# Lightning attention and a Mish feed-forward in one kernel: the place of two "turns" of group 3, and of one key decay in the head

## The chip, the cores and the metric

The kernel runs on one core of a Trainium2 chip. The metric is the device time of one execution in microseconds (us); several executions are timed and their median is given. A profile is one more execution, recorded by the hardware profiler. The engines are called PE (matrix multiplication; PEld is its weight load), DVE (VectorE), ACT (ScalarE), POOL (GpSimd) and SP (SyncE, which only issues DMAs here). ACT and POOL issue DMAs too, each in its own instruction order: a DMA whose conditions are not met holds up everything behind it on the issuing engine.

## The reference

Four batches, eight heads, 768 positions, head size 64. Causal attention without softmax and with a decay per head goes block by block over the positions and carries a 64 x 64 state per head; its result, laid out as 3072 tokens x 512, goes through a feed-forward layer with the Mish function. Cut to what matters:

```python
for b in range(nb):                          # blocks of positions
    intra = einsum('bhic,bhjc->bhij', qb, kb) * Dmask
    intra = einsum('bhij,bhjd->bhid', intra, vb)
    inter = einsum('bhid,bhde->bhie', qb * lam_pow, kv_state)
    out[:, :, sl] = intra + inter
    kv_state = lam_block * kv_state + einsum('bhsd,bhse->bhde', kb * rev_pow, vb)
x = out.transpose(0, 2, 1, 3).reshape(3072, 512)
h = x @ w_in                                 # 512 -> 2048
g = h * tanh(softplus(h))                    # Mish
return g @ w_out                             # 2048 -> 512
```

## The kernel before

**Groups and chunks.** The 768 positions are cut into six groups of 128 (`n`, 0 to 5; the "fourth group" is n = 3). A group has four chunks, one per batch: chunk `i = 4 n + b` is 128 positions of batch `b`, all eight heads. Below, k12 or q12 means the key or query part of chunk 12, v12 its values; chunks 12 to 15 are group 3.

**Attention of a chunk.** `load_k`, `load_q`, `load_v` (L62 to L79) fetch a chunk from HBM as fp16; POOL issues them. `scale_k` (L263) multiplies the keys by their decay and gives `ktil`; it runs on POOL for groups 1 to 4 and on DVE for groups 0 and 5. Groups 0 and 1 are transposed on PE (`first_t`, `first_s`, `first_o`); `first_t(c)` of group 1 reads `ktil`. From group 2 on, `turn(i)` (L270) does the same job by DMA: `scale_k(i)`, then two transposing DMAs issued by SP, `qn` to `qraw` and `ktil` to `kraw` (L275). `pair_s` (L312) multiplies `kraw` by `qraw` for two chunks at a time, `pair_o` (L342) forms the attention output, and SP issues two more transposing DMAs from `xtok` into `xt` (L361), the layout that the feed-forward reads. `pair_a` updates the state: PE, then DVE (`raw`), then POOL (`w`, L305).

**Feed-forward of a group.** `mm1_unit` (L383) makes one 128 x 512 piece of the hidden layer in a PSUM tile `ph` (two buffers) and ACT applies Mish into `hsg` (L387). `mm2_unit` (L429) makes a quarter of one batch's output in `po`; after the fourth quarter ACT copies `po` to `osb` (L427, three buffers) and itself issues the output DMA (L424, 256 KB). Both instructions stand on ACT, one behind the other.

**Periods.** After a head in which groups 0 and 1 go through attention and `mm1`, the main loop (L533) runs n = 1 to 5. A period is a list of "units" of feed-forward work on PE (n = 1: the 32 `mm2_unit`s of groups 0 and 1; n = 2 to 5: 16 `mm1_unit`s, then 16 `mm2_unit`s), and `todo` (filled by `at`) says what is put behind which unit: the attention of group n+1 (`pair_s`, `pair_o`, `pair_a`), and the loads and turns of group n+2. Nothing is reordered later: what each engine does stands in the order in which this code is written out. Loads are held back by `behind` (L367), a one-element POOL copy from a result that must be there first ("tick").

**DMA names.** The DMAs that SP and ACT issue take eight completion semaphores in turn, in program order. A DMA that takes a semaphore waits until the DMA that had it before has landed. In the instruction lists below, `DMAHW5_49` among an instruction's waits is such a semaphore, and `DMASW...` those of the loads.

**The head's loads.** Behind the weights, POOL issues the twelve loads of group 1 (L487 to L493) with the key decays of its chunks between them (`scale_k(B)` is chunk 4), then the loads of `w_out` and the first loads of group 2.

Of the kernel before, what the change touches and what calls it, by code (L numbers as in the profile page):

```python
# [13 lines left out]
def bc(ap, axis, n):  # L14
    shape = list(ap.shape)
    shape.insert(axis, n)
    return ap.unsqueeze(axis).broadcast_to(shape)
# [3 lines left out]
def kernel(  # L21
# [11 lines left out]
    B, H, S, D = q.shape  # L33
# [9 lines left out]
    NVB = 8  # L43
    NT = 2
# [13 lines left out]
    def chunk_rows(t, i):  # L58
        n, b = divmod(i, B)
        return t[b, :, n * C : (n + 1) * C, :].rearrange("h p c -> p h c")  # L60

    def load_k(i):  # L62
        if i == 0:
            kn[i] = const.tile([128, H, D], F32, name="kn0")
            nc.sync.dma_start(out=kn[i], in_=chunk_rows(k, i))
            return
        kn[i] = loads.tile([128, H, D], F16, name="kn", tag="kn")
        nc.gpsimd.dma_start(out=kn[i], in_=chunk_rows(k, i))  # L68

    def load_q(i):  # L70
        if i == 0:
            qn[i] = const.tile([128, H, D], F32, name="qn0")
            nc.scalar.dma_start(out=qn[i], in_=chunk_rows(q, i))
            return
        qn[i] = loads.tile([128, H, D], F16, name="qn", tag="qn")
        nc.gpsimd.dma_start(out=qn[i], in_=chunk_rows(q, i))  # L76

    def load_v(i):
        nc.gpsimd.dma_start(out=vz[i % NVB][:, :, 0:D], in_=chunk_rows(v, i))  # L79
# [32 lines left out]
    def load_chunk(i):  # L112
        load_k(i)
        load_q(i)
        load_v(i)
# [147 lines left out]
    def scale_k(i):  # L263

        t = work.tile([128, H, D], F16, name="ktil", tag="ktil", bufs=8)
        (nc.vector if i < B or i >= (NG - 1) * B else nc.gpsimd).tensor_tensor(  # L266
            out=t, in0=kn[i], in1=bc(lk, 2, D), op=ALU.mult)
        ktil[i] = t
# [98 lines left out]
    def behind(src):  # L367
        nc.gpsimd.tensor_copy(tick, src)  # L368

    hsg = [None] * NG  # L370
# [113 lines left out]
    for hp in range(2):  # L484
        rs = slice(64 * hp, 64 * hp + 64)
        nc.vector.tensor_copy(lbm[rs, :, rs], bc(lbc[rs, :], 2, D))
    for i in range(B, NVB - 1):  # L487
        load_chunk(i)
    scale_k(B)
    load_k(NVB - 1)  # L490
    scale_k(B + 1)
    load_q(NVB - 1)
# [11 lines left out]
    for u in range(NKI):  # L504
# [7 lines left out]
        if u in (6, 7, 8, 10):  # L512
            i = {6: 4, 7: 5, 8: 6, 10: 7}[u]
# [19 lines left out]
    for n in range(NT - 1, NG):  # L533
        dense = [(mm2_unit, m, b, part) for m in ((0, 1) if n < NT else (n,))
                 for b in range(B) for part in range(WS)]
        if n >= NT:
            dense = [(mm1_unit, n, ni) for ni in range(NKI)] + dense
        todo = {}

        def at(u, f, *args):  # L540
            todo.setdefault(u, []).append((f, args))

        if n + 1 < NG:
            pairs = []
            for b in (0, 2):
                s = Pair()
                s.n, s.b = n + 1, b
                pairs.append(s)
            steps = (((9, pair_s, 0), (13, pair_o, 0), (14, pair_a, 0),
                      (16, pair_s, 1), (20, pair_o, 1), (28, pair_a, 1)) if n < NT else  # L550
                     ((4, pair_s, 0), (8, pair_o, 0), (9, pair_a, 0),
                      (13, pair_s, 1), (17, pair_o, 1), (25, pair_a, 1)))
            for u, f, b in steps:
                at(u, f, pairs[b])
        if n + 2 < NG:
            c = (n + 2) * B
            loads_ = [(f, c + b) for b in range(B) for f in (load_k, load_q)]
            loads_ += [(load_v, c + b) for b in range(B)]
            for x, (f, i) in enumerate(loads_):
                if n >= NT:  # L560
                    u = (1, 2, 3, 5, 6, 8, 10, 11, 12, 13, 14, 15)[x]
                    at(u, lambda u=u: behind(hsg[n][0:1, u, 0:1]))
                else:
                    u = 7 + x // 2 * 4
                    if x % 2 == 0:
                        at(u, lambda: behind(last_out[0][0:1, 0:1]))
                at(u, f, i)
            for b, u in enumerate((21, 22, 24, 26) if n < NT else (18, 19, 21, 23)):
                at(u, turn, c + b)
        for u, (fn, *args) in enumerate(dense):  # L570
            fn(*args)
            for f2, args in todo.get(u, ()):
                if args and isinstance(args[0], Pair):
                    args[0].spare = "po" if u < NKI - 1 and n >= NT else "ph"
                f2(*args)
# [30 lines left out]
```

## Time and profile before

| | |
|---|---|
| time, median of 3 runs | 214.5 us (213.99, 214.5, 215.1) |
| the profiled execution's own time | 214.28 us |
| its span in the profile | 212.5 us |
| granted PE clock | 1.0 |
| PE busy | 203.4 us, 96% of the span |
| POOL, ACT, DVE busy | 112.8, 86.3, 72.4 us |

All times inside the profile count from the start of the span. The span is 1.78 us shorter than the execution's time. Matmul ends in the profile are modelled, so a stall of PE is best read from starts. Period n = 1 begins at about 55 us, n = 2 at 86.15 us, n = 3 at 119.6 us.

### The profile page before, as it was taken

What the parts mean: (1) busy time and instruction counts of PE and PEld (TensorE: products, weight loads), DVE (VectorE), ACT (ScalarE), POOL (GpSimd) and SP (SyncE); (2) the same over time, 40 slices, a digit from 0 to 9 for tenths busy, and PEclk for the clock granted to TensorE, in tenths of its full rate; (3) what the DMA queues carried; (4) which work ended last, traced back from release to release, by engine and by line L of the source; (5) the groups of instructions that cost most, each with busy time, mean ns of one, the idle gap of its engine ahead of it and who ended that gap; (6) DMA issues with size and microseconds to landing.
All of it is one profiled execution on the core that took longest, in us unless ns stands there. A gap on an engine that the chain in (4) does not pass through costs nothing.

```text
span 212.5 us, 4185 instructions
## 1 busy us (share of the span) xinstructions
PE 203.4 (96%) x1680; PEld 111.4 (52%) x1680; DVE 72.4 (34%) x149; ACT 86.3 (41%) x146; POOL 112.8 (53%) x166
## 2 busy tenths in 40 slices
PE   7798999999999999699999999999999999999994
PEld 2465547999645545255454455545454544444442
DVE  6867736740005822044422044462042510000000
ACT  5664566656321121355412355412356321566120
POOL 7997399989934879768994169924000000000000
PEclk9999999999999999999999999999999999999999
DMA  9999999999999999999998799997702042100112
GB/s 130 138 150 192 187 155 116 185 187 156 145 169 233 147 132 174 165 232 87 108 142 201 181 91 86 107 180 156 193 10 47 2 102 99 51 0 0 52 49 99
DMA packets 109894, 26.76 MB, mean 126 GB/s; under 512 B 102578, under 2 KB 106930, under 8 KB 109874
## 3 DMA queue, kind: packets, MB, share of 16 engines
q0 software_dynamic: 78080, 13.37, 84.4%
q1 hardware_dynamic: 27296, 6.63, 19.4%
q10 hardware_dynamic: 4498, 6.49, 9.4%
q8 instruction: 13, 0.21, 0.4%
q14 instruction: 7, 0.06, 0.1%
HBM read 27.26 MB, written 6.29 MB: 158 GB/s over the span
## 4 chain that ended last, share of the span: by engine, by line
PE 77%; POOL 10%; DMA 8%; issue 2%; ACT 1%; DVE 0%; ACTq 0%; POOLq 0%
PE po L412 34%; PE ph L380 27%; PE ph L398 6%; DMA win<-in_moe_w_in_dram 6%; DMA kraw<-ktil 3%; POOL vz L79 3%; PE pS L324 2%; POOL qn L76 2%; PE pO L351 2%; POOL kn L68 2%; PE pv L291 1%; POOL ktil L266 1%; POOL win L92 1%; PE pO L330 1%; PE pO L256 1%
## 5 line engine op out<-in xcount | busy, mean ns | idle before, releaser
L412 PE MATMUL po<-wout,hsg 128*128 128x512 f16 (+2 forms) x400 | 85.6, 371 | 0.0
L380 PE MATMUL ph<-xt,win 128*128 128x512 f16 (+2 forms) x332 | 73.9, 371 | 2.3 <-ACT hsg L387 2.1
L387 ACT ACTIVATE hsg<-ph 128x512 f16<-128x512 f32 x80 | 47.5, 597 | 31.3 <-PE ph L380 30.5
L412 PEld LDWEIGHTS <-hsg 128*128 128x128 f16 x400 | 37.9, 98 | 41.9
L380 PEld LDWEIGHTS <-win 128*128 128x128 f16 x332 | 30.8, 98 | 36.3 <-issue 3.4
L427 ACT ACTIVATE osb<-po 128x512 f32<-128x512 f32 (+1 forms) x24 | 14.2, 593 | 75.5 <-PE po L412 65.1
L339 DVE TENSOR_TENSOR sb<-pS,maskT 128x512 f16<-128x512 f32 x32 | 19.9, 682 | 52.6 <-PE pS L324 52.6
L305 POOL TENSOR_TENSOR w<-raw,lbm 128x256 f16<-128x256 f32 x32 | 22.2, 724 | 10.8 <-DVE raw L303 10.7
L68 POOL DMA_DIRECT2D kn<-in_k_dram x23 | 21.2, 923 | 4.0 <-DMA win<-in_moe_w_in_dram 1.7
L79 POOL DMA_DIRECT2D vz<-in_v_dram x24 | 21.6, 904 | 2.0 <-DMA win<-in_moe_w_in_dram 2.0
L76 POOL DMA_DIRECT2D qn<-in_q_dram x23 | 20.7, 901 | 3.6 <-DMA win<-in_moe_w_in_dram 1.6
L303 DVE TENSOR_TENSOR raw<-pv,w 128x256 f32<-128x256 f32 x32 | 11.4, 414 | 16.4 <-PE pv L291 16.4
L266 POOL TENSOR_TENSOR ktil<-kn,lk 128x512 f16<-128x512 f16 x16 | 16.5, 1052 | 0.3
L357 DVE TENSOR_TENSOR xtok<-pO,lqt 128x512 f16<-128x512 f32 x16 | 10.3, 686 | 15.9 <-PE pO L351 15.9
L398 PE MATMUL ph<-xt,win 128*128 128x128 f16 x256 | 15.3, 219 | 0.0
L398 PEld LDWEIGHTS <-win 128*128 128x128 f16 x256 | 14.5, 98 | 0.1
L421 DVE COPY osb<-po 128x128 f32<-128x128 f32 x1 | 0.3, 291 | 38.7 <-PE po L412 38.7
L402 ACT ACTIVATE hsg<-ph 128x512 f16<-128x512 f32 x16 | 9.6, 597 | 6.9 <-PE ph L398 6.9
L368 POOL COPY tick<-hsg 1x1 f16<-1x1 f16 x24 | 4.2, 177 | 8.7 <-ACT hsg L387 8.6
L163 PE MATMUL busy<-kzero 128*128 128x512 f16 x18 | 7.6, 516 | 1.2 <-DVE kzero L149 1.2
L291 PEld LDWEIGHTS <-ktil 128*128 128x128 f16 x80 | 5.5, 98 | 2.7 <-issue 0.3
L291 PE MATMUL pv<-vz,ktil 128*128 128x128 f16 x80 | 6.8, 219 | 0.2 <-DVE sb L241 0.2
(68 smaller groups left out, 117.2 us busy)
## 6 DMA issues: line engine op xcount, KB each, us to landing
out_dram<-osb ACTq DMA_DIRECT2D x23, 256.0 KB, 3.0
vz<-in_v_dram POOLq DMA_DIRECT2D x24, 128.0 KB, 4.8
kn<-in_k_dram POOLq DMA_DIRECT2D x23, 128.0 KB, 4.2
qn<-in_q_dram POOLq DMA_DIRECT2D x23, 128.0 KB, 4.4
wout<-in_moe_w_out_dram POOLq DMA_DIRECT2D x4, 512.0 KB, 8.7
win<-in_moe_w_in_dram POOLq DMA_DIRECT2D x3, 512.0 KB, 10.3
kn<-in_k_dram SPq DMA_DIRECT2D x1, 256.0 KB, 3.2
qn<-in_q_dram ACTq DMA_DIRECT2D x1, 256.0 KB, 3.9
```

Of the source, the lines that this page charges most:

```text
L68: nc.gpsimd.dma_start(out=kn[i], in_=chunk_rows(k, i))
L76: nc.gpsimd.dma_start(out=qn[i], in_=chunk_rows(q, i))
L79: nc.gpsimd.dma_start(out=vz[i % NVB][:, :, 0:D], in_=chunk_rows(v, i))
L266: (nc.vector if i < B or i >= (NG - 1) * B else nc.gpsimd).tensor_tensor(out=t, in0=kn[i], in1=bc(lk, 2, D), op=ALU.mult)
L291: nc.tensor.matmul(pv[:, j, :].rearrange("p (a e) -> p a e", a=2), ktil[i][:, 2 * j : 2 * j + 2, :].rearrange("p h c -> p (h c)"), vz[i % ...
L305: nc.gpsimd.tensor_tensor(out=w_new, in0=raw, in1=lbm[:, hs, :], op=ALU.mult)
L339: nc.vector.tensor_tensor(out=s.sb[x][t], in0=pS[x][t], in1=bc(maskT, 1, JP), op=ALU.mult)
L380: nc.tensor.matmul(ph_t[ni][:, lo:hi], win_t(ni, kc), xt[n][:, kc, lo:hi], start=(kc == 0), stop=(kc == NKC - 1))
L387: nc.scalar.activation(hsg[n][:, ni, :], ph_t.pop(ni), AF.Mish)
L398: nc.tensor.matmul(ph[:, u, :], win_t(w * s + u, kc), xt[n][:, kc, b * C : (b + 1) * C], start=(kc == 0), stop=(kc == NKC - 1),)
L412: nc.tensor.matmul(po[:, lo:hi], hsg[n][:, ki, b * C : (b + 1) * C], wout[part][:, kk, lo:hi], start=(ki == 0), stop=(ki == NKI - 1),)
L427: nc.scalar.activation(o, i, AF.Copy)
```

## The change

Two edits.

1. In period n = 1 the four turns of group 3 stood behind units 21, 22, 24 and 26. Now only the first two (chunks 12 and 13) stand there, behind units 21 and 23. The other two (chunks 14 and 15) stand behind unit 0 of period n = 2, after a tick that waits for the first Mish result of that period. Periods n = 2 and later keep their own turns at 18, 19, 21, 23.
2. In the head, `scale_k(B)`, the decay of chunk 4, stands directly behind `load_k(6)`, ahead of `load_q(6)` and `load_v(6)`; before, it stood behind them.

```diff
-    for i in range(B, NVB - 1):
+    for i in range(B, NVB - 2):
         load_chunk(i)
+    load_k(NVB - 2)
     scale_k(B)
+    load_q(NVB - 2)
+    load_v(NVB - 2)
     load_k(NVB - 1)
     scale_k(B + 1)
...
+        if n == NT:
+            at(0, lambda: behind(hsg[n][0:1, 0, 0:1]))
+            at(0, turn, (n + 1) * B + 2)
+            at(0, turn, (n + 1) * B + 3)
         if n + 2 < NG:
...
-            for b, u in enumerate((21, 22, 24, 26) if n < NT else (18, 19, 21, 23)):
+            for b, u in enumerate((21, 23) if n < NT else (18, 19, 21, 23)):
                 at(u, turn, c + b)
```

On ACT no instruction moves, but the semaphores do, because the turns now take them later in the program. These are the last two output DMAs of period n = 1 (batches 2 and 3 of group 1) and the first Mish of period n = 2, before:

```order
L427 ACTIVATE osb<-po 128x512 [waits DMAHW0_49,PE_49,Pool_49]
L424 DMA out_dram<-osb 128x512 [waits DMAHW5_49,Activation_49]
L427 ACTIVATE osb<-po 128x512 [waits DMAHW1_49,PE_49,Pool_49]
L424 DMA out_dram<-osb 128x512 [waits DMAHW6_49,Activation_49]
L387 ACTIVATE hsg<-ph 128x512 [waits PE_49] x16
```

and now:

```order
L427 ACTIVATE osb<-po 128x512 [waits DMAHW0_49,PE_49,Pool_49]
L424 DMA out_dram<-osb 128x512 [waits DMAHW2_49,Activation_49]
L427 ACTIVATE osb<-po 128x512 [waits DMAHW1_49,PE_49,Pool_49]
L424 DMA out_dram<-osb 128x512 [waits DMAHW3_49,Activation_49]
L387 ACTIVATE hsg<-ph 128x512 [waits PE_49] x16
```

The two DMAs waited for the holders of semaphores 5 and 6; now they wait for the holders of 2 and 3. Who these are shows SP's list at the same place, which in its order is the same before and now. Before: the two `xt` transposes of group 2's second pair, then q12, k12, q13, k13, q14, k14, q15, k15 (each takes the semaphore that it waits for):

```order
L361 DMA_TRANSPOSE xt<-xtok 128x4x128 [waits DMAHW2_49,DVE_49]
L361 DMA_TRANSPOSE xt<-xtok 128x4x128 [waits DMAHW3_49]
L275 DMA_TRANSPOSE qraw<-qn 128x4x128 [waits DMAHW4_49,DMASW5_49,PE_49]
L275 DMA_TRANSPOSE kraw<-ktil 128x4x128 [waits DMAHW5_49,Pool_49]
L275 DMA_TRANSPOSE qraw<-qn 128x4x128 [waits DMAHW6_49,DMASW7_49,PE_49]
L275 DMA_TRANSPOSE kraw<-ktil 128x4x128 [waits DMAHW0_49,Pool_49]
L275 DMA_TRANSPOSE qraw<-qn 128x4x128 [waits DMAHW1_49,DMASW1_49,PE_49]
L275 DMA_TRANSPOSE kraw<-ktil 128x4x128 [waits DMAHW2_49,Pool_49]
L275 DMA_TRANSPOSE qraw<-qn 128x4x128 [waits DMAHW3_49,DMASW3_49,PE_49]
L275 DMA_TRANSPOSE kraw<-ktil 128x4x128 [waits DMAHW4_49,Pool_49]
```

So the two output DMAs waited for k12 (semaphore 5) and q13 (semaphore 6); now they wait for the two `xt` transposes (2 and 3). On SP itself k14, q15 and k15 take 4, 5 and 6 in place of 2, 3 and 4, in the same places.

POOL, around the end of period n = 1. The `ktil` rows are the decays of the turns, `tick` the holds, `vz` the loads of v12 to v15, `w` the last state update of the period; the lines with + and - are what the change adds and removes:

```order
-L266 TENSOR_TENSOR ktil<-kn,lk 128x512 x2
+L266 TENSOR_TENSOR ktil<-kn,lk 128x512
 L368 CAST tick<-osb 1x1
 L79 DMA vz_73<-in_v_dram 128x8x64
 L79 DMA vz_74<-in_v_dram 128x8x64
-L266 TENSOR_TENSOR ktil<-kn,lk 128x512 x2
+L266 TENSOR_TENSOR ktil<-kn,lk 128x512
 L368 CAST tick<-osb 1x1
```

and, behind the four `w` rows, at the start of period n = 2:

```order
 L305 TENSOR_TENSOR w_171<-raw,lbm 128x256
 L305 TENSOR_TENSOR w_173<-raw,lbm 128x256
+L368 COPY tick<-hsg 1x1
+L266 TENSOR_TENSOR ktil<-kn,lk 128x512 x2
 L368 COPY tick<-hsg 1x1
 L68 DMA kn<-in_k_dram 128x8x64
```

Two decays moved from ahead of v14 and v15 to ahead of the first load of group 4, with one tick more. And POOL in the head:

```order
 L68 DMA kn<-in_k_dram 128x8x64
+L266 TENSOR_TENSOR ktil<-kn,lk 128x512
 L76 DMA qn<-in_q_dram 128x8x64
 L79 DMA vz_75<-in_v_dram 128x8x64
-L266 TENSOR_TENSOR ktil<-kn,lk 128x512
 L68 DMA kn<-in_k_dram 128x8x64
```

The decay of chunk 4 moved up past the loads q6 and v6.

## The prediction

> **What bounds the kernel now.** I read the page first, then PE's waits, then the chain that ended last, then the timeline of the stretches in which PE waits. The first row of the page, and PE's five longest waits in the trace (columns: who, for whom, us in total, times, longest):
>
> ```profile
> PE 203.4 (96%) x1680; PEld 111.4 (52%) x1680; DVE 72.4 (34%) x149; ACT 86.3 (41%) x146; POOL 112.8 (53%) x166
> PE ph L380 <- ACT hsg L387: 2.1, 2, 1.9
> PE busy L163 <- DVE kzero L149: 1.2, 1, 1.2
> PE pq L217 <- DVE q L451: 0.7, 1, 0.7
> PE pk L217 <- POOL ktil L266: 0.4, 1, 0.4
> PE pO L256 <- DVE sb L241: 0.4, 1, 0.4
> ```
>
> PE bounds the kernel: work taken off another engine is worth nothing unless PE waits for it. Two of these waits lie where the change works: 1.9 us for a Mish, and 0.4 us for `ktil`. The first is at the start of period n = 2. The timeline there (columns: start, length, engine and line, what; in brackets the idle time before):
>
> ```profile
> 82.50 0.60 ACT L427 ACTIVATE osb<-po 128x512 f32<-128x512 f32 x1 [2.85 <-PE po L412]
> 86.15 1.89 PE L380 MATMUL ph<-xt,win 128*128 128x512 f16 x8
> 87.75 0.38 ACTq L424 DMA_DIRECT2D out_dram<-osb  x1
> 88.25 0.60 ACT L427 ACTIVATE osb<-po 128x512 f32<-128x512 f32 x1 [5.15 <-POOL w L305]
> 88.87 0.35 ACTq L424 DMA_DIRECT2D out_dram<-osb  x1
> 89.27 1.09 ACT L387 ACTIVATE hsg<-ph 128x512 f16<-128x512 f32 x2 [0.43 <-ACT osb L427]
> 89.92 2.75 PE L380 MATMUL ph<-xt,win 128*128 128x512 f16 x12 [1.88 <-ACT hsg L387]
> ```
>
> ACT copied batch 2's output by 83.10, but its DMA left only at 87.75; behind it stood the copy of batch 3, that one's DMA, and the first Mish (89.27). PE had filled both `ph` buffers and waited. The view puts ACT's idle time down to POOL's `w`, but the instruction that was blocked is the DMA. By the list of ACT it waits for semaphore 5, which k12 held, and the chain agrees: k12 leaves at 81.85 and lands 5.82 us later, at 87.67. The chain also shows the same place in a later period, where nothing blocks ACT (start, length, what), and the two places at which group 3's transposed keys are first used:
>
> ```profile
> 81.85 5.82 DMA kraw<-ktil
> 92.67 0.55 PE pS L324 x16
> 102.25 0.55 PE pS L324 x16
> 150.97 1.73 PE ph L380 x8
> 152.69 0.03 issue
> 152.72 2.75 PE ph L380 x12
> ```
>
> At 150.97 eight matmuls take 1.73 us and the ninth starts 1.75 us after the first. At 86.15 it starts 3.77 us after. So the stall, read from starts, costs 3.77 - 1.75 = 2.02 us.
>
> **Term 1: the output DMAs' new wait.** They now wait for the two `xt` transposes. When those land (SP's issue of each, and the time from issue to landing; then q13 and q14, for below):
>
> ```profile
> L361 SPq DMA_TRANSPOSE xt<-xtok x1: 1190/1190/1190, 77.7 to 77.7; - x1
> DMA to landing us min/median/max: 5.4/5.4/5.4
> L361 SPq DMA_TRANSPOSE xt<-xtok x1: 1309/1309/1309, 78.9 to 78.9; - x1
> DMA to landing us min/median/max: 5.4/5.4/5.4
> L275 SPq DMA_TRANSPOSE qraw<-qn x1: 1295/1295/1295, 83.3 to 83.3; - x1
> DMA to landing us min/median/max: 4.7/4.7/4.7
> L275 SPq DMA_TRANSPOSE qraw<-qn x1: 1213/1213/1213, 86.0 to 86.0; - x1
> DMA to landing us min/median/max: 5.6/5.6/5.6
> ```
>
> The first `xt` lands at 77.7 + 5.4 = 83.1, just as the copy ends (82.50 + 0.60); the second, also 5.4 us after its issue, at 84.3, well before the copy of batch 3 can end. PE starts unit 0 at 86.15, that is batch 3's last matmul has gone out; copy 0.60, DMA issue 0.35 and the gaps around them put the first Mish at about 87.2 and its end at 87.8, where the ninth matmul would be due at 86.15 + 1.75 = 87.9. The whole stall goes: -2.02 us. Nothing earlier in the period is touched, so 83.1 should hold. Bounds: 0, if `xt` landed as late as k12 does now, and -2.02.
>
> **Term 2: k13 may become late.** Once PE no longer waits, the next thing that it needs from this queue is k13, for the first `pair_s` at 92.67, now 92.67 - 2.02 = 90.65; the second chunk's eight matmuls come half of 0.55 us later, at 90.9. k13's own landing the views do not give, but q13 lands at 83.3 + 4.7 = 88.0 and q14 at 86.0 + 5.6 = 91.6, and SP issues k13 between them; half way is 89.8. That alone leaves 1.1 us. But the change also puts other traffic in front: batch 2's output write leaves 4.6 us sooner (83.1, not 87.75) and batch 3's about 1.8 us sooner, and v14 and v15 leave about 0.9 us sooner, as one `ktil` (half of the 2.06 us pair) no longer stands ahead of them. The page's row of the output queue, and POOL's rows:
>
> ```profile
> q10 hardware_dynamic: 4498, 6.49, 9.4%
> 82.07 2.06 POOL L266 TENSOR_TENSOR ktil<-kn,lk 128x512 f16<-128x512 f16 x2
> 84.19 1.82 POOL L79 DMA_DIRECT2D vz<-in_v_dram  x2
> 86.01 2.77 POOL L305 TENSOR_TENSOR w<-raw,lbm 128x256 f16<-128x256 f32 x4
> 91.25 0.94 POOL L68 DMA_DIRECT2D kn<-in_k_dram  x1 [0.57 <-issue]
> ```
>
> 9.4% of 212.5 us over 24 writes is 0.83 us of all 16 DMA engines per write (estimate). With batch 2's write wholly ahead, k13 lands at 89.8 + 0.83 = 90.6, in time; with both, at 91.5, and PE waits 0.6 us. Lower bound 0; upper bound 91.6 + 2 x 0.83 - 90.9 = 2.4 us, which takes back the whole of term 1. I take +0.3 us, the middle of the two cases of one and of two writes.
>
> The Trainium skill, "DMA: Bandwidth & Descriptors", section "Queues, rings and completion order", says that each DMA engine takes the queues that have work in turn, packet by packet. By that rule the transposes, sharing with the loads now, would share three ways while output writes are in flight, so the last 5 us or so before k13's landing would stretch by up to half, to 7.5 us or so, and k13 would land at about 92.2: an estimate that lies inside the bounds above, at a wait of 1.3 us in place of my 0.3.
>
> **Term 3: the moved turns.** Two decays, three transposes (k14, q15, k15; q14 waits for nothing on POOL and leaves as before at 86.0) and one tick go later. POOL is free for them when the `w` rows end, now 0.9 us sooner at 87.9; tick and two decays take it to 90.1. The first tick of group 4's loads follows, and with the 0.57 us gap k16 leaves at about 90.9, against 91.25 now: no cost. SP issues k14 at about 89.2 and each next one 1.3 us on, so k15 leaves at about 91.9. This is from all 16 `kraw` transposes:
>
> ```profile
> DMA to landing us min/median/max: 2.4/3.6/6.3
> ```
>
> At 3.6 to 6.3 us k15 lands between 95.5 and 98.2. It is needed at 102.25 - 2.02 + 0.3 = 100.5 or later: cost 0, slack 2.3 us at the worst row. What hides it is the nine `mm1` units between the two `pair_s`. Behind the three on SP stand only the `xt` transposes of the first pair, which are ready long after 94.
>
> **Term 4: the head.** Rows of POOL and PE:
>
> ```profile
> L68 POOL DMA_DIRECT2D kn<-in_k_dram x1: 1015/1015/1015, 15.2 to 15.2; - x1
> DMA to landing us min/median/max: 12.2/12.2/12.2
> 26.86 0.88 POOL L76 DMA_DIRECT2D qn<-in_q_dram  x1 [1.62 <-DMA win<-in_moe_w_in_dram]
> 27.40 1.89 PE L380 MATMUL ph<-xt,win 128*128 128x512 f16 x8
> 28.62 1.05 POOL L266 TENSOR_TENSOR ktil<-kn,lk 128x512 f16<-128x512 f16 x1
> 29.73 0.40 PE L217 MATMUL pk<-ident,ktil 128*128 128x128 f16 x4 [0.44 <-POOL ktil L266]
> 33.39 1.06 POOL L266 TENSOR_TENSOR ktil<-kn,lk 128x512 f16<-128x512 f16 x1
> 35.62 0.40 PE L217 MATMUL pk<-ident,ktil 128*128 128x128 f16 x4
> ```
>
> PE's eight matmuls from 27.40 end their turn at 27.40 + 1.73 = 29.13, and `first_t(4)` starts at 29.73: 0.60 us late, for the `ktil` that ends at 29.67. k4's data land at 15.2 + 12.2 = 27.4, so the decay could start at about 27.7 (the load q6 took 0.3 us from its release to its start) and end at 28.8, ahead of 29.13: up to -0.60 us. But q6 and v6 go behind it, and POOL's list from there on shifts by the delay: before, chunk 6's decay started 33.39 - 26.86 = 6.53 us after q6, with the same instructions between; now it starts that long after 27.7, at 34.2, and ends at 35.3. PE wants it at 35.62 - 0.60 = 35.0. So about 0.3 us comes back: I take -0.30 us, with bounds -0.60 and 0. Later loads leave some 0.8 us late, w_out's first (used at 55 us) and group 2's among them; those have microseconds to spare.
>
> **The sum.** -2.02 + 0.30 + 0 - 0.30 = -2.02 us. Against the profiled execution, 214.28 gives 212.26; that execution stands 0.22 us under the median 214.5, so by the median 212.5. I predict 212.4.
>
> **Rivals.** (a) k13 stalls PE for about 1.3 us, not 0.3 (term 2, up to its bound of 2.4): 214.4 - 2.02 + 1.3 - 0.3 = 213.4, spread 212.8 to 214.3. For it: loads, transposes and writes all want the DMA engines between 83 and 90. Against it: of the transposes only those ahead of k13 count, and these are the same as before. The Trainium skill's rule in term 2 points this way too. (b) The change does not free ACT: `xt` lands late, since it lands at 83.1 with nothing to spare, and the stall stays in good part. Then 213.7 to 214.5. Against it: a microsecond's delay of `xt` costs nothing, since ACT has nothing else to do until 86. (c) Slower: the moved turns come too late. One mechanism, k15's landing at the second `pair_s`: PE would wait from 100.5 on, and the kernel is slower from a landing after 100.5 + 2.0, that is 10.6 us after its issue at 91.9, against 6.3 us in the worst row; at 12 us it would be 1.4 us slower than now, 215.9.
>
> **How the numbers follow.** A measurement of this kernel can tell about 0.5%, here 1.07 us, from no change. The forecast, 211.8 to 212.8, gets 0.55; (a) 0.27; (b) 0.12; (c) 0.06. Faster by more than 0.5% means under 213.4: all of the forecast and 0.22 of (a), 0.77. Within: the rest of (a) and (b), 0.17. Slower: (c), 0.06. The range runs from 211.6 (term 4 whole, term 2 zero: 214.4 - 2.62 = 211.8, and 0.2 for the spread of the runs) to 213.8, which takes in most of (a) and leaves out (c) and most of (b).
>
> **What would show it.** Right: PE's wait for the Mish at the start of n = 2 gone, the two output DMAs issued at about 83.2 and 87; k13's wait at the first `pair_s` of group 3 under 0.6 us; no wait at the second; the wait for `ktil` at 29.7 gone, a shorter one at 35. Wrong: a new wait of PE at L324 of more than 1 us (a), ACT still blocked at L424 near 83 to 87 (b), or a wait at the second `pair_s` (c).

## The result

The changed kernel takes 212.92 us, the kernel before 214.23 us (medians of 19 executions each). The ratio is 0.9938, with a 95% interval of 0.9917 to 0.9959: by the ratio 1.33 us faster, between 0.88 and 1.78. The ratios here and below leave out executions more than 1.5% above the fastest of their kernel (here one on each side), which the medians keep. The profiled execution of the changed kernel took 213.17 us, with a span of 211.4 us.

PE's row of the page, then its longest waits and the two that answer to those shown of before (who, for whom, us in total, times, longest):

```profile
PE 203.0 (96%) x1680; PEld 111.1 (53%) x1680; DVE 72.1 (34%) x149; ACT 86.2 (41%) x146; POOL 113.1 (53%) x167
```

```profile
PE busy L163 <- DVE kzero L149: 1.2, 1, 1.2
PE ph L380 <- DMA win<-in_moe_w_in_dram: 1.2, 2, 0.9
...
PE ph L380 <- ACT hsg L387: 0.2, 1, 0.2
```

The wait for the Mish was 2.1 us in total and is 0.2 us; the wait for the `ktil` of chunk 4 is no longer in the list. PE has still the same work: 203.0 us busy against 203.4. The timeline at the start of period n = 2 (start, length, engine and line, what; in brackets the idle time before), ACT and PE:

```profile
83.28 0.60 ACT L427 ACTIVATE osb<-po 128x512 f32<-128x512 f32 x1 [2.85 <-PE po L412]
83.91 0.34 ACTq L424 DMA_DIRECT2D out_dram<-osb  x1
86.93 4.66 PE L380 MATMUL ph<-xt,win 128*128 128x512 f16 x20
87.18 0.60 ACT L427 ACTIVATE osb<-po 128x512 f32<-128x512 f32 x1 [3.30 <-PE po L412]
87.81 0.34 ACTq L424 DMA_DIRECT2D out_dram<-osb  x1
88.19 1.26 ACT L387 ACTIVATE hsg<-ph 128x512 f16<-128x512 f32 x2 [0.42 <-PE ph L380]
91.52 0.62 PE L324 MATMUL pS<-qraw,kraw 64*128 64x128 f16 x16
101.10 0.62 PE L324 MATMUL pS<-qraw,kraw 64*128 64x128 f16 x16
```

Batch 2's DMA leaves 0.03 us after its copy ends (83.91), where it stood until 87.75 before. The first Mish starts 1.26 us after period 2 does, not 3.12 us, and the twenty matmuls run as one group. Inside that group the chain that ended last shows the ninth matmul:

```profile
88.84 2.75 PE ph L380 x12
```

It starts 1.91 us after the first (86.93), against 3.77 us before. Period 2 itself started 0.78 us later in this execution (86.93, not 86.15). 0.78 - 1.86 = -1.08 us, and the two profiled executions differ by 214.28 - 213.17 = 1.11 us: the place where the change works accounts for the difference, and the later start arose in the head (last section).

SP's rows for the moved transposes, k14, q15 and k15, and the time to landing of the last:

```profile
90.21 1.19 SPq L275 DMA_TRANSPOSE kraw<-ktil  x1
91.50 1.22 SPq L275 DMA_TRANSPOSE qraw<-qn  x1
92.81 1.39 SPq L275 DMA_TRANSPOSE kraw<-ktil  x1
```

```profile
L275 SPq DMA_TRANSPOSE kraw<-ktil x1: 1388/1388/1388, 92.8 to 92.8; - x1
DMA to landing us min/median/max: 6.0/6.0/6.0
```

k15 lands at 98.8, and the second `pair_s` wants it at 101.1.

### The profile page after: what moved, and what is told of

Read it like the earlier page. It is cut to its first block, busy times and chain, and to the rows that moved or that the text cites. A ratio compares the mean times of both kernels' runs of the same rounds, so it can differ in the third digit from the quotient of the medians.

```text
span 211.4 us, 4188 instructions
## 1 busy us (share of the span) xinstructions
PE 203.0 (96%) x1680; PEld 111.1 (53%) x1680; DVE 72.1 (34%) x149; ACT 86.2 (41%) x146; POOL 113.1 (53%) x167
## 4 chain that ended last, share of the span: by engine, by line
PE 81%; POOL 10%; DMA 6%; issue 1%; DVE 0%; POOLq 0%
PE po L412 39%; PE ph L380 27%; PE ph L398 6%; DMA kn<-in_k_dram 6%; POOL vz L79 2%; PE pS L324 2%; POOL qn L76 2%; PE pO L351 2%; POOL kn L68 2%; PE pv L291 2%; POOL ktil L266 2%; POOL win L92 1%; POOL win L95 1%; PE pO L330 1%; PE pO L256 1%
```

## The experiments

Each is told against the kernel before, unless it says otherwise. "Edit 1" is the moving of the turns, "edit 2" the decay in the head. "Ninth matmul" is the time from the first matmul of period 2 to the ninth, the measure of the stall.

**Each edit alone.** The first kernel has edit 1 only; it was run twice, on two chips.

```
+        if n == NT:
+            at(0, lambda: behind(hsg[n][0:1, 0, 0:1]))
+            at(0, turn, (n + 1) * B + 2)
+            at(0, turn, (n + 1) * B + 3)
...
-            for b, u in enumerate((21, 22, 24, 26) if n < NT else (18, 19, 21, 23)):
+            for b, u in enumerate((21, 23) if n < NT else (18, 19, 21, 23)):
```

> The first edit alone (two turns moved; the head as before). Theory H: the moved turns are worth the whole stall, about 2.0 us, and the head edit takes part of it back by making group 2's loads late; then this kernel is 2.0 us faster than before (ratio 0.990 to 0.991), faster than both edits together, and w_out and group 2's loads land as early as before. Theory K (rival): the moved turns themselves are worth only about 1.3 us over many executions, because k13 lands late in some; then the ratio is 0.993 to 0.995, and both edits together are no slower than this one.

> The first edit alone, once more, for a second time and profile: ratio 0.9945 as measured (0.992 to 0.997), the start of period 2 between 85.3 and 87.0 us with the head's weights, and the execution's time following that start one for one.

Measured: 213.03 against 213.80 us, ratio 0.9945 (0.9915 to 0.9975), and the second time 212.70 against 213.87 us, ratio 0.9938 (0.9920 to 0.9956). That is as much as both edits together brought (0.9938). The ninth matmul comes after 1.92 and 1.91 us. The profiled execution of the first:

```profile
86.08 4.66 PE L380 MATMUL ph<-xt,win 128*128 128x512 f16 x20
90.68 0.62 PE L324 MATMUL pS<-qraw,kraw 64*128 64x128 f16 x16
91.14 0.40 PE L330 MATMUL pO<-w,qraw 64*128 64x64 f16 x16
```

and of the second, where `pair_s` takes 0.83 us instead of 0.62 because its second half waits 0.21 us for k13:

```profile
91.34 0.83 PE L324 MATMUL pS<-qraw,kraw 64*128 64x128 f16 x16
92.01 0.40 PE L330 MATMUL pO<-w,qraw 64*128 64x64 f16 x16
```

The second kernel has edit 2 only:

```
-    for i in range(B, NVB - 1):
+    for i in range(B, NVB - 2):
         load_chunk(i)
+    load_k(NVB - 2)
     scale_k(B)
+    load_q(NVB - 2)
+    load_v(NVB - 2)
```

> The second edit alone (chunk 4's decay ahead of q6 and v6; turns as before). Theory H: PE gains 0.4 us at first_t(4), but w_out and group 2's loads land 2 us or more later than before and the first pair_s of group 2 waits for k9; time between 0.3 us faster and 1 us slower than before (ratio 0.9985 to 1.005). Theory K: it keeps the 0.3 to 0.6 us gained in the head (ratio 0.997 to 0.9985).

Measured: 213.64 against 213.80 us, ratio 0.9986 (0.9949 to 1.0024). By time alone this tells nothing. The trace tells more when it is read from a common start. The eight `mm1` matmuls directly ahead of `first_t(4)` serve for that, since up to them no edit changes anything that PE waits for; before, they began at 27.40 and `first_t(4)` at 29.73. With edit 2 alone they, `first_t(4)`, and the first `pair_s` and `pair_o` of the main loop (chunks 8 and 9) are:

```profile
27.62 1.89 PE L380 MATMUL ph<-xt,win 128*128 128x512 f16 x8
29.34 0.39 PE L217 MATMUL pk<-ident,ktil 128*128 128x128 f16 x4
63.24 0.40 PE L324 MATMUL pS<-qraw,kraw 64*128 64x128 f16 x8
63.84 0.40 PE L324 MATMUL pS<-qraw,kraw 64*128 64x128 f16 x8 [0.20 <-DMA kraw<-ktil]
64.07 0.40 PE L330 MATMUL pO<-w,qraw 64*128 64x64 f16 x16
```

and the same `pair_s` and `pair_o` before:

```profile
63.64 0.62 PE L324 MATMUL pS<-qraw,kraw 64*128 64x128 f16 x16
64.09 0.40 PE L330 MATMUL pO<-w,qraw 64*128 64x64 f16 x16
```

`first_t(4)` starts 1.72 us after the eight matmuls, not 2.33, and `pair_s` 35.62 us after them, not 36.24: 0.6 us is gained and still there at 63 us. Then the second half of `pair_s` waits for k9's transpose. Read from starts, `pair_o` follows `pair_s` by 0.83 us and not by 0.45, so 0.38 us is lost here (the 0.20 of the view counts from a modelled end). Period 2 starts 58.50 us after the eight matmuls, not 58.75, so 0.25 us is left. The plain times, 86.12 and 86.15, hide this, since the eight matmuls themselves began 0.22 us later in this execution.

What makes k9 late is open. `w_out`'s loads leave POOL from 34.8 on with edit 2 alone, from 34.4 on before; but with edit 1 alone, whose head is unchanged, k9's transpose left SP later still in the first profile (58.32, against 57.05 with edit 2 alone) and landed at 63.7, about 0.1 us ahead of its use. So k9 had little to spare there without edit 2, and with it PE comes 0.6 us sooner.

**Is it the semaphore?** Edit 1 moves the turns and with them the order in which DMAs take semaphores. To tell the two apart, this kernel has edit 1 and three 32-byte DMAs on SP which do nothing but take a semaphore each, so that batch 2's output DMA again takes the one that k12 held. The turns stay moved.

```
+    spare8 = [const.tile([1, H], F32, name=f"spare8{x}") for x in range(3)]
+    def tiny(x):
+        nc.sync.dma_start(out=spare8[x], in_=lam.unsqueeze(0))
...
+            if n < NT:
+                for x in range(3):
+                    at(21, tiny, x)
```

> The first edit alone, with three DMAs of 32 bytes issued by SP behind the first turn of group 3, which only take semaphores: the output DMA of batch 2 then waits for k12 again, though the turns of chunks 14 and 15 stay put off. Semaphore theory: the stall of PE at the start of period 2 comes back, 1.8 to 2.0 us, and the time is that of before (ratio 0.998 to 1.002). Rival, that moving the DMA traffic and POOL's decays is what freed ACT: no stall, time as with the first edit alone (ratio 0.990 to 0.994).

Measured: 213.86 against 213.80 us, ratio 1.0001 (0.9969 to 1.0033). The whole gain is gone. The timeline:

```profile
82.43 0.60 ACT L432 ACTIVATE osb<-po 128x512 f32<-128x512 f32 x1 [2.86 <-PE po L417]
87.54 0.34 ACTq L429 DMA_DIRECT2D out_dram<-osb  x1
88.00 0.60 ACT L432 ACTIVATE osb<-po 128x512 f32<-128x512 f32 x1 [4.97 <-PE ph L385]
86.08 1.89 PE L385 MATMUL ph<-xt,win 128*128 128x512 f16 x8
89.67 2.75 PE L385 MATMUL ph<-xt,win 128*128 128x512 f16 x12 [1.69 <-ACT hsg L392]
```

```profile
L275 SPq DMA_TRANSPOSE kraw<-ktil x1: 1222/1222/1222, 81.6 to 81.6; - x1
DMA to landing us min/median/max: 5.9/5.9/5.9
```

k12 lands at 81.6 + 5.9 = 87.5, and batch 2's DMA leaves at 87.54. The ninth matmul comes 3.59 us after the first, with the turns where the change put them. The stall is the semaphore's, then, and moving the turns helps only by changing who held it. Note that the view puts the 4.97 us down to PE's `ph` here and to POOL's `w` in the kernel before; neither is what ACT waited for.

**Two other ways to the same end.** The first leaves all turns where they were and puts the two output DMAs of period 1 on POOL's queue, whose DMAs do not take these eight semaphores:

```
-            mm2_out(n, b, po, 0, DMO, act_copy, nc.scalar)
+            mm2_out(n, b, po, 0, DMO, act_copy, nc.gpsimd if n == 1 and b >= 2 else nc.scalar)
```

> The kernel before with all four turns of group 3 where they were, but the output DMAs of batches 2 and 3 in period 1 issued by POOL, whose DMAs take other semaphores. Semaphore theory: ACT is not held, PE's wait at the start of period 2 goes (the ninth matmul 1.9 us after the first, in place of 3.4 to 3.8), ratio 0.990 to 0.995, as with the first edit alone. Rival, that the early transposes themselves hold things up: PE still waits, ratio 0.998 to 1.002.

Measured: 212.06 against 213.87 us, ratio 0.9903 (0.9881 to 0.9926), which rests on four executions, 211.65 to 212.20. It was run beside the second run of edit 1 alone (0.9938); the two intervals overlap between 0.9920 and 0.9926.

```profile
85.98 4.48 PE L380 MATMUL ph<-xt,win 128*128 128x512 f16 x20
86.23 0.60 ACT L427 ACTIVATE osb<-po 128x512 f32<-128x512 f32 x1 [3.30 <-PE po L412]
87.04 0.60 ACT L387 ACTIVATE hsg<-ph 128x512 f16<-128x512 f32 x1 [0.22 <-PE ph L380]
90.39 0.62 PE L324 MATMUL pS<-qraw,kraw 64*128 64x128 f16 x16
```

ACT has no DMA to issue between the copy and the Mish, so the Mish starts 1.06 us after period 2, not 1.26, and the ninth matmul comes after 1.72 us. That is 0.19 us better than the change, and `pair_s` did not wait for k13 in this execution (in that of edit 1 beside it it did, 0.21 us). Apart from one kernel below whose lead did not come a second time, this is the lowest ratio of the study; it beats the kernel before; its lead of 0.3% over the changed kernel (0.9938, and 0.9934 in a second measurement below) is not settled by these runs. The traces bear out 0.2 us of it at most: from the start of period 2 to the end of the span this kernel takes 124.4 us, and edit 1 alone 124.4 and 124.7.

The second puts off only chunk 15's turn:

```
+            at(0, turn, (n + 1) * B + 3)
...
-            for b, u in enumerate((21, 22, 24, 26) if n < NT else (18, 19, 21, 23)):
+            for b, u in enumerate((21, 22, 24) if n < NT else (18, 19, 21, 23)):
```

> The first edit with one turn put off, not two (chunk 15 alone; chunks 12 to 14 behind units 21, 22 and 24). Batch 2's output DMA then waits for q12 and batch 3's for k12. Semaphore theory: batch 3's DMA leaves when k12 lands, at about 87.5, the first Mish at about 88.0, so the ninth matmul of period 2 comes 2.6 to 2.9 us after the first: about half of the stall stays, ratio 0.995 to 0.997. Rival: the stall goes or stays whole.

Measured, in six executions: 212.63 against 213.87 us, ratio 0.9940 (0.9917 to 0.9962).

```profile
85.54 0.34 ACTq L424 DMA_DIRECT2D out_dram<-osb  x1
86.50 0.60 ACT L427 ACTIVATE osb<-po 128x512 f32<-128x512 f32 x1 [3.30 <-PE po L412]
87.30 0.36 ACTq L424 DMA_DIRECT2D out_dram<-osb  x1
88.35 2.75 PE L380 MATMUL ph<-xt,win 128*128 128x512 f16 x12 [0.21 <-ACT hsg L387]
```

The ninth matmul comes 2.10 us after the first (86.25), not 2.6 to 2.9: batch 2's DMA is blocked until 85.54, but ACT has nothing else to do until batch 3's copy at 86.50, and batch 3's is held up for 0.20 us (87.10 to 87.30). By the trace one turn put off is worth nearly as much as two (2.10 us against 1.91), since what counts is only whether the holders land before ACT's next work.

**Where edit 2's gain goes.** If its decay costs POOL's loads their place, the same decay on DVE, which is 34% busy, should keep the early start and leave POOL's loads alone. Edit 1 and chunk 4's decay on DVE, behind unit 9 of group 0's `mm1`:

```
-        (nc.vector if i < B or i >= (NG - 1) * B else nc.gpsimd).tensor_tensor(
+        (nc.vector if i <= B or i >= (NG - 1) * B else nc.gpsimd).tensor_tensor(
...
-    scale_k(B)
...
+        if u == 9:
+            scale_k(B)
```

> The first edit, and chunk 4's decay on DVE (behind the state update of chunk 3) in place of POOL, so that POOL never waits for k4 and issues q6 and everything after it 1 us earlier than the kernel before. Theory H: the wait of PE at first_t(4) goes, no load becomes late, and the gain is 2.0 + 0.6 = 2.6 us (ratio 0.988). Theory K: 1.3 + 0.6 = 1.9 us (ratio 0.991).

Measured first, in six executions: 211.89 against 213.80 us, ratio 0.9891 (0.9846 to 0.9936), which looked like a better kernel. So it was run again, beside both edits:

> The first edit with chunk 4's decay on DVE, once more, beside both edits. If it is the better version: ratio 0.987 to 0.991 again, and under that of both edits by 0.2% to 0.5%; no wait for k9 in the profile. If the first measurement was luck: 0.993 to 0.995, as both edits.

> Both edits, once more, beside the next kernel on the same chip and for a second profile. Ratio 0.9938 as measured, period 2 starting between 86.0 and 87.0 us with the head's weights, and a wait of 0.2 to 0.4 us for k9 at the first pair_s of group 2 if the head edit makes that late each time.

Measured: 0.9924 (0.9895 to 0.9953) with the decay on DVE, 0.9934 (0.9905 to 0.9962) with both edits as they are, against the same runs of before. The lead was not there a second time. With POOL's output DMAs and the decay on DVE together:

> All turns of group 3 where they were, the output DMAs of batches 2 and 3 in period 1 issued by POOL, and chunk 4's decay on DVE. If the two add up: 0.9903 for the output DMAs and 0.2 to 0.5 us (the wait for ktil in the head, up to 0.6 us) for the decay, ratio 0.988 to 0.9895. If the decay's place is worth nothing by itself: 0.990 to 0.992.

the ratio was 0.9914 (0.9887 to 0.9941), no better than POOL's output DMAs alone (0.9903). By the times, the decay's place is worth nothing that these runs can tell. By the traces it is worth something: from the eight matmuls to the start of period 2 PE takes 58.13 us in all three profiles with the decay on DVE, 58.50, 58.55 and 58.29 in the three with edit 2, and 58.72 to 58.81 in five with the unchanged head (58.49 in a sixth, the kernel with one turn put off, where chunk 4's `ktil` was less late; the two kernels of the next paragraph, which have more work there, are left out). On DVE the whole 0.6 us is kept, with edit 2 it is 0.2 to 0.5. That is 0.1% to 0.3% of the time, no more than the width of the intervals. The wait for k9 that was expected of both edits is there in one of their two profiles.

**Why less than the stall?** Edit 1 takes 1.49 to 1.86 us of stall away, by the traces, and brings 1.18 and 1.33 us (0.0055 x 213.80 and 0.0062 x 213.87; by the intervals 0.53 to 1.82 and 0.94 to 1.71, so the shortfall may be noise). Nothing of it is paid back later: from the start of period 2 to the end of the span the four profiles with the stall take 125.9 to 126.4 us, the ten in which it is gone or nearly gone 124.4 to 124.8. One theory for what lies ahead of period 2: the stall ended at k12's landing, a time that did not hang on PE, so it also absorbed delays that come up ahead of it, and without it these come through. Both kernels of this pair have four matmuls more (0.86 us) behind unit 13 of group 0's `mm1`, whose result only overwrites the same sums; the first has no other edit, the second has edit 1 too.

```
+        if n == 0 and ni == 13:
+            for kc in range(NKC):
+                nc.tensor.matmul(ph_t[ni], win_t(ni, kc), xt[n][:, kc, :],
+                                 start=(kc == 0), stop=(kc == NKC - 1))
```

> The kernel before, with unit 13 of group 0's mm1 multiplied twice (4 more matmuls, 0.86 us of PE in the head, the result the same). Absorption theory: k12's landing is set by what the DMA engines have queued and not by PE, so it stays at 87.2 to 87.9 us while period 2 starts 0.86 us later; the stall shrinks from 2.0 to about 1.2 us and the time grows by 0 to 0.3 us (ratio 1.000 to 1.0015). Rival, that k12 follows PE through xtok and xt: landing at about 88.5, stall still 2.0, ratio 1.004.

> The first edit alone, with the same 4 more matmuls. With no stall left to hide them they cost their whole 0.86 us: ratio to the kernel before 0.9945 + 0.004 = 0.9985 (with the 0.9945 measured for the first edit alone). If the absorption theory fails for some other reason, for instance that DMA waits further on hide them, the ratio stays near 0.9945.

Measured: ratios 1.0028 (1.0007 to 1.0049) and 0.9969 (0.9942 to 0.9996). The delay costs the kernel before 0.0028 x 213.99 = 0.6 us; against edit 1 alone (0.9938 and 0.9945) it costs 0.0024 to 0.0031 of 213.99, 0.5 to 0.7 us. Both pay about the same, so the theory is not supported. The intervals, 0.5 us to either side, do not rule out a small part. In the first kernel's trace k12 lands at 82.3 + 5.7 = 88.0, 0.3 us later than before: its issue moves with PE's work, so the stall's end is less fixed than the theory had it. The stall is no shorter either: the ninth matmul comes after 3.58 us.

## Why the prediction was right, and where its sizes were off

The forecast was 212.4 us, with 211.6 to 213.8 as its range; the median is 212.92. The reading of the stall was right and its size was taken too large; in the head one step failed. The gain came out 0.69 us smaller than the forecast 2.02; the time missed by less, 0.5 us, only because the forecast started from 214.4, by three executions, where nineteen gave 214.23.

**Term 1, the stall (-2.02).** Its mechanism is shown by the three 32-byte DMAs, which bring the whole stall back with the turns still moved. Its size was off, twice. The ninth matmul was put at 1.75 us after the first, from a later period where ACT has no output DMA to issue; in the changed kernel it is 1.91 us, with 0.2 us of waiting left. And 3.77 us was one execution: three other executions with the stall in full show 3.40 (edit 2 alone), 3.59 (the tiny DMAs) and 3.58 us (the late matmuls). Against 1.91 the stall costs 1.49 to 1.86 us, not 2.02. This is the term that was mis-sized.

**Term 2, k13 (+0.30, bounds 0 to 2.4).** The place was right, and the wait was never more than forecast: PE waits at the second half of the first `pair_s` for 0 in three profiles (the changed kernel twice, edit 1 once) and for 0.21 to 0.27 us in four others with edit 1. That the earlier output writes cause it, as the prediction had it, no run separates. Rival (a), 1.3 us, did not come, nor the sharing by three that an estimate from the Trainium skill's rule ("DMA: Bandwidth & Descriptors", "Queues, rings and completion order") gave k13. With a wait of at most 0.27 us in seven profiles, the traces do not agree with that estimate, which stretches k13's last 5 us by half.

**Term 3, the moved turns (0).** Right: k15 left at 92.81, landed at 98.8 and was wanted at 101.10. Rival (c) needed a landing 10.6 us after issue, and it took 6.0.

**Term 4, the head (-0.30).** Its size was right by the traces, though the times can't tell it, and one of its steps failed. The changed kernel's eight matmuls, `first_t(4)`, chunk 6's `first_t`, and the first `pair_s` and `pair_o` of the main loop:

```profile
28.38 1.89 PE L380 MATMUL ph<-xt,win 128*128 128x512 f16 x8
30.11 0.39 PE L217 MATMUL pk<-ident,ktil 128*128 128x128 f16 x4
36.19 0.40 PE L217 MATMUL pk<-ident,ktil 128*128 128x128 f16 x4
64.20 0.84 PE L324 MATMUL pS<-qraw,kraw 64*128 64x128 f16 x16
64.88 0.40 PE L330 MATMUL pO<-w,qraw 64*128 64x64 f16 x16
```

`first_t(4)` follows the eight matmuls by 1.73 us, so the whole wait of 0.60 us is gone, as in the other two profiles with edit 2. Chunk 6's decay was to take 0.3 us of it back; it takes 0.21 and 0.17 us with both edits and nothing with edit 2 alone. The step that failed is the last, that later loads "have microseconds to spare": k9's transpose holds up the first `pair_s` by 0.23 us here and by 0.38 us with edit 2 alone, though not in the changed kernel's second profile. Period 2 is reached 0.20, 0.25 and 0.46 us sooner than before, counted from the eight matmuls, around the 0.30 of the forecast; that a loss which was left out and a loss taken too large about cancel is luck.

Whether the decay's new place makes POOL's loads later is not shown. It does make POOL wait for k4:

```profile
28.56 1.04 POOL L266 TENSOR_TENSOR ktil<-kn,lk 128x512 f16<-128x512 f16 x1 [2.42 <-DMA kn<-in_k_dram]
```

and q10's load leaves at 46.40, where it left at 43.54 before; but with edit 1 alone, where the decay stands in its old place, it left at 45.17 and 45.81.

**The sum.** By the traces 1.2 to 1.9 us are gained behind the start of period 2 (the stall, less k13's wait) and 0.2 to 0.5 us in the head, some 1.8 us in the middle. Measured were 1.33 (0.88 to 1.78) and, the second time, 1.41 us (0.81 to 2.03). That both lie at the small end may be chance or something ahead of the eight matmuls, which begin anywhere from 27.00 to 28.38 us in these profiles; it is not explained, and the absorption that was tried does not account for it.

**The order of the semaphores.** They were said to be taken in the program's order. That holds only nearly: q14 takes semaphore 1 ahead of the output DMAs' 2 and 3, though its turn stands behind unit 0 of period 2. The holders were read from the instruction lists and so were right.

## What to carry to other kernels

An output DMA on a compute engine's queue can wait not only for its data but for whoever held its completion semaphore before; when such an engine idles for microseconds ahead of a DMA whose data are ready, look up that holder rather than the releaser that a view names, and free the engine by changing who holds the semaphore or which queue issues the DMA. A stall whose end is set by a transfer differs from one execution to the next, so size it from several places or executions and not from one. And before work is pulled forward, follow each transfer behind it to its first user, far down as well: of 0.6 us won at 29 us, only 0.2 to 0.5 us was left at 86 us. To see such a gain at all, count from a point that the change can't have moved, and not from the start of the span.

## What was not expected of the hardware

Two executions of one kernel can part by over 1 us within the first 30 us. Two profiled executions of the same changed kernel took 213.17 and 211.56 us, and period 2 starts 1.64 us apart, at 86.93 in the first and in the second at:

```profile
85.29 4.66 PE L380 MATMUL ph<-xt,win 128*128 128x512 f16 x20
```

The eight matmuls ahead of `first_t(4)`, which began at 28.38 in the first, began at 27.00 in the second:

```profile
27.00 1.89 PE L380 MATMUL ph<-xt,win 128*128 128x512 f16 x8
```

So 1.38 us are there already at this point. PE had waited 1.2 us for the loads of `w_in` in the first (the second row of its waits above) and not at all in the second. Most of the 1.61 us between the two executions has nothing to do with the change, so a gain of 1 us in this kernel can be read from two profiles only after the start of the stretch has been subtracted.

Issuing a DMA costs the issuing engine as well: 0.34 us of ACT for an output write, of which 0.2 us was left as PE's waiting in the changed kernel and none in the one with POOL's output DMAs.
